# One-hot products that stream four tokens' rows instead of one

## The chip, the cores and the metric

The kernel runs on one core of a Trainium2 chip. A core has TensorE (matrix products, called PE in the profile, with its weight loads counted as PEld), VectorE (DVE), ScalarE (ACT), GpSimd (POOL) and the queue of SyncE (SP), which issues transfers. The metric is the device time of one execution in microseconds; of several runs the median is given.

## The reference

A layer-normalised input `xn` of 2048 tokens by 512 features goes through two branches, whose results are added to the input:

```
xn = layernorm(x)
out = x + attention(xn, wq, wk, wv, wo) + experts(xn, w_q, k1, k2, u, v)
```

The attention has 32 query heads of 16 features and a single key and value head. The expert branch has 32 heads too. For each token and head it scores two sets of 64 keys, takes the two best of each, combines them to four candidates, and keeps the two best of these, so a token picks 64 of 4096 experts with gates `g`:

```
s1 = q1 @ k1.T ; s2 = q2 @ k2.T
top_e, top_s = best 2 of (t1[i] + t2[j]) at expert i1[i] * 64 + i2[j]
g   = softmax(top_s)
act = gelu(xn @ u[top_e])
out = sum over picks of g * act * v[top_e]
```

## The kernel before

The 2048 tokens are four groups of 512. Attention runs through the whole kernel after a start of about 160 us. Its loop (`att_steps`, line 1138) has 280 iterations. Each one issues on TensorE four score products (line 327, tile `sc`), sixteen products with the values (line 341, tile `pv`), four more score products, and then `fill`, which takes work of the expert branch from a generator until a budget per iteration is spent. ScalarE takes an exponential of each pair of score products (line 330, tile `pt`), which the value products of the next iteration need.

The expert branch has two forms. For token groups 0 and 1, the picked rows of `u` and `v` are gathered by GpSimd (line 976), and VectorE takes the dot products (line 988) and adds the weighted rows (line 1023); this runs beside everything else, a fixed few of them in each iteration. For token groups 2 and 3 (`dense`, line 656) there is no gather: the gates of a token are spread out to a dense table over all 4096 experts, and all experts are multiplied by TensorE (lines 733 and 861).

That spreading is where the change lies. An expert's number is split into 128 rows (`oa`) and 32 blocks (`ob`). For each group `q` of `TB = 16` tokens, VectorE makes in `onehot(q)` a table `oa` of shape 128 x 128 x 16 in f16 (line 783), in which one element of each pick and token is 1, and a table `ob` of shape 128 x 32 x 16 in f16 (line 785), which line 786 multiplies by the gates. The partition axis of both holds the picks of a token, 128 of them since each gate is carried in a high and a low part. TensorE then makes for each token one product over the picks: `oa[:, :, i]` is loaded as weights, `ob[:, :, i]` is streamed, 32 rows, and the result is the token's 128 x 32 table of gates in 32 columns of the PSUM tile `p` (tile `pg`, line 815). The innermost axis of both tables is the token, so neighbouring elements of one token lie 16 elements apart. When the 16 tokens of a group are done, ScalarE copies `p` out in two halves (line 820), and transfers take them to DRAM.

The tables are made two groups ahead (`onehot(q + 2)` stands ahead of the products of `q`); `ob` has three buffers, and `oa` shares the eight buffers of the tag `wk`. The PSUM tiles of tag `x` have three buffers. A group of 16 tokens is put down with a cost of 2.0, and an iteration takes up to 4.0 (`MOST`), so most iterations hold two groups. There are 32 groups in each of the two dense token groups, thus 64 in all, and 1024 products on line 815. The order of every engine's instructions is written out by hand (`manual_schedule`), and each engine runs its own in that order.

The results of line 815 are written with `start=True, stop=True`: each product overwrites its output columns and adds to nothing.

## Time and profile before

| | us |
|---|---|
| median of three runs | 1927.19 |
| lowest and highest run | 1919.88, 1936.14 |
| the profiled execution | 1931.19 |
| its span, first to last instruction | 1929.5 |

The profiled execution's mean granted TensorE clock is 0.980. Durations in what follows are from that one execution, whose time is 1.7 us above its span and 4.0 us above the median.

In the lines of the profile an engine's busy time is the union of its instructions' times; since matmuls are pipelined, TensorE counts as busy while a product drains, even if the array does little. PEclk and the column behind the engines in the answers by windows are the granted clock: 1.00 is full speed. The chain of waits follows the work that ended last back in time; its rows are start, length, engine, tile, line and number of instructions. In the rows by line, the first figure behind the bar is busy time in us, the second the mean duration of one instruction in ns, then the idle time just before them.

### The profile page before, as it was taken

What the parts mean: (1) busy time and instruction counts of PE and PEld (TensorE: products, weight loads), DVE (VectorE), ACT (ScalarE), POOL (GpSimd) and SP (SyncE); (2) the same over time, 40 slices, a digit from 0 to 9 for tenths busy, and PEclk for the clock granted to TensorE, in tenths of its full rate; (3) what the DMA queues carried; (4) which work ended last, traced back from release to release, by engine and by line L of the source; (5) the groups of instructions that cost most, each with busy time, mean ns of one, the idle gap of its engine ahead of it and who ended that gap; (6) DMA issues with size and microseconds to landing.
All of it is one profiled execution on the core that took longest, in us unless ns stands there. A gap on an engine that the chain in (4) does not pass through costs nothing.

```text
span 1929.5 us, 35007 instructions
## 1 busy us (share of the span) xinstructions
PE 1865.4 (97%) x10990; PEld 995.2 (52%) x10990; DVE 1633.0 (85%) x6381; ACT 1294.3 (67%) x1803; POOL 693.5 (36%) x920
## 2 busy tenths in 40 slices
PE   6879999999999999999999999999999999999998
PEld 4544444555555544555555454555555555555553
DVE  6626788889998976999999897899988879999994
ACT  3336666655557887877877555555578877888873
POOL 1202334334453213343444354344522124344430
PEclk9989999999999989999999999999999999999999
DMA  7856878887673668799889977877645778899882
GB/s 269 300 202 229 291 263 294 287 294 277 231 268 121 216 213 260 248 283 292 267 288 308 353 278 241 295 243 264 216 138 194 267 222 291 271 284 284 283 274 83
DMA packets 245724, 491.14 MB, mean 255 GB/s; under 512 B 93972, under 2 KB 106260, under 8 KB 245532
## 3 DMA queue, kind: packets, MB, share of 16 engines
q0 software_dynamic: 73728, 268.47, 41.4%
q1 hardware_dynamic: 170568, 219.56, 34.9%
q8 instruction: 88, 1.44, 0.3%
q10 hardware_dynamic: 1236, 0.82, 0.1%
q14 instruction: 104, 0.85, 0.1%
HBM read 427.41 MB, written 56.07 MB: 251 GB/s over the span
## 4 chain that ended last, share of the span: by engine, by line
PE 84%; DVE 3%; ACT 2%; issue 1%; DMA 1%; another core or an unknown queue 0%; SPq 0%; ACTq 0%; DVEq 0%
PE pv L341 23%; PE psc L531 18%; PE sc L327 17%; PE pact L733 10%; PE pout L861 9%; PE pg L815 2%; PE pwo L434 2%; ACT pt L330 2%; PE pw L487 2%; DVE oh L783 1%; DMA wk<-dw 1%; DVE xa L1023 1%; DMA wqt<-in_wqT_dram 0%; PE pwt L494 0%; PE pwl L409 0%
## 5 line engine op out<-in xcount | busy, mean ns | idle before, releaser
L330 ACT ACTIVATE pt<-sc 128x1024 f32<-128x1024 f32 x1024 | 994.4, 1026 | 459.2 <-PE sc L327 405.9
L976 POOL DMA_INDIRECT g<-in_uv_dram,idx x512 | 555.0, 1084 | 1009.5 <-DVE xa L1023 531.9
L341 PE MATMUL pv<-pt,vaug 128*32 128x512 f32 x4096 | 508.9, 615 | 0.0
L531 PE MATMUL psc<-wk,xt 128*128 128x512 f32 x1536 | 390.9, 402 | 6.6 <-DVE wk L497 3.5
L327 PE MATMUL sc<-qa,kaug 64*128 64x512 f32 x2048 | 387.0, 453 | 7.7 <-ACT pt L330 6.9
L1023 DVE SCALAR_TENSOR_TENSOR xa<-g,w,xa 128x512 f32<-128x512 f32 x512 | 371.5, 744 | 0.1
L988 DVE CUSTOM_DVE_ANT_0 g<-g,xa 128x512 f32<-128x512 f32 x512 | 335.2, 680 | 6.6 <-DMA g<-in_uv_dram,idx 6.6
L531 PEld LDWEIGHTS psc<-wk,xt 128*128 128x128 f32 x1536 | 279.4, 189 | 110.5 <-issue 40.3
L327 PEld LDWEIGHTS sc<-qa,kaug 64*128 64x128 f32 x2048 | 157.1, 187 | 326.1 <-ACT pt L330 194.3
L341 PEld LDWEIGHTS pv<-pt,vaug 128*32 128x32 f32 x4096 | 108.8, 111 | 255.7 <-issue 254.1
L546 DVE FIND_INDEX8 i<-m,psc 128x8 uint32<-128x64 f32 x1024 | 206.2, 220 | 0.0
L733 PE MATMUL pact<-xt,wk 128*128 128x512 f32 x768 | 196.0, 400 | 0.0
L861 PE MATMUL pout<-wk,wd 128*128 128x512 f32 x768 | 194.9, 402 | 0.2 <-DVE wd L919 0.2
L544 DVE MAX8 m<-psc 128x8 f32<-128x64 f32 x1024 | 146.1, 213 | 41.2 <-PE psc L531 40.0
L861 PEld LDWEIGHTS pout<-wk,wd 128*128 128x128 f32 x768 | 140.8, 188 | 47.4 <-issue 5.5
L733 PEld LDWEIGHTS pact<-xt,wk 128*128 128x128 f32 x768 | 139.4, 188 | 48.6 <-issue 17.9
L864 DVE TENSOR_TENSOR da<-da,pout 128x512 f32<-128x512 f32 x128 | 82.7, 678 | 10.1 <-PE pout L861 8.6
L698 DVE TENSOR_TENSOR wk<-rw,wk 128x512 fp32r<-128x512 f32 x128 | 84.7, 682 | 7.1 <-ACT wk L697 7.1
L783 DVE TENSOR_TENSOR oh<-oh 128x2048 f16<-128x2048 f16 x64 | 78.0, 1219 | 2.3 <-PE pg L815 1.7
L815 PEld LDWEIGHTS <-oh 128*128 128x128 f16 x1024 | 68.4, 163 | 13.6 <-issue 4.8
L815 PE MATMUL pg<-oh 128*128 128x32 f16 x1024 | 73.7, 246 | 0.8 <-DVE oh L786 0.7
L697 ACT CAST wk<-rw 128x512 fp32r<-128x512 f32 x128 | 74.0, 632 | 0.0
(159 smaller groups left out, 1356.4 us busy)
## 6 DMA issues: line engine op xcount, KB each, us to landing
wk<-dw SPq DMA_DIRECT2D x96, 512.0 KB
wqt<-in_wqT_dram SPq DMA_DIRECT2D x32, 512.0 KB
dw<-wk SPq DMA_DIRECT2D x32, 512.0 KB
rw<-in_ub_dram SPq DMA_DIRECT2D x64, 256.0 KB
rw<-in_vb_dram SPq DMA_DIRECT2D x64, 256.0 KB
gy<-dg SPq DMA_DIRECT2D x64, 256.0 KB
qa<-dqh SPq DMA_DIRECT2D x128, 64.0 KB
g<-in_uv_dram,idx POOLq DMA_INDIRECT x512
```

The costliest lines, as they stand in the source:

```text
L327: nc.tensor.matmul(p[:, b, :], kaug[o:o + 64, kc * P:(kc + 1) * P], QA[u][o:o + 64, i, :], start=True, stop=True)
L330: nc.scalar.activation(pt, p, AF.Exp, scale=SCALE)
L341: nc.tensor.matmul(PV[u][32 * j:32 * j + 32, :], vaug[:, kc, :], pt[:, b, :], start=kc == 0, stop=kc == 15)
L531: nc.tensor.matmul(p, XT[k][:, a, j * P:(j + 1) * P], WC[n_][k][:, bb, :], start=n == 0, stop=n == 11)
L544: nc.vector.max(m8[:, jb, s, :], p[:, s * E:(s + 1) * E])
L546: nc.vector.max_index(i8[:, jb, s, :], m8[:, jb, s, :], p[:, s * E:(s + 1) * E])
L733: nc.tensor.matmul(p, us[:, a, k * P:(k + 1) * P], XT[k][:, c, :], start=n == 0, stop=n == 11)
L815: nc.tensor.matmul(p[:, i * NB:(i + 1) * NB], oa[:, :, i], ob[:, :, i], start=True, stop=True)
L861: nc.tensor.matmul(p, wd[0][:, a, j * P:(j + 1) * P], vs[:, c, :], start=n == 0, stop=n == 5)
L976: nc.gpsimd.indirect_dma_start(out=gt, out_offset=None, in_=uv, in_offset=bass.IndirectOffsetOnAxis(ap=IDX[ph, c, ti][:, s:s + 1], axis=0))
L988: nc.vector.tensor_tensor_reduce(u, u, XN[TPH * ph + ti], scale=1.0, scalar=0.0, op0=OP.mult, op1=OP.add, accum_out=a[:, i:i + 1])
L1023: nc.vector.scalar_tensor_tensor(acc, v, w[:, i:i + 1], acc, op0=OP.mult, op1=OP.add)
```

## The change

Each product of line 815 streams, instead of the 32 rows of its own token, those of its token and of the next three of the group, as far as the group reaches: 128 rows for the first thirteen tokens, then 96, 64 and 32. It writes as many columns of `p`. The columns of the later tokens then hold a product of their `ob` with the wrong `oa`, until the later token's own product, which comes behind on the same engine, overwrites them. After the sixteenth product every token's columns hold its own result, as before.

```diff
+WIDE = 4
...
             p = xtile("pg")
             for i in range(TB):
-                nc.tensor.matmul(p[:, i * NB:(i + 1) * NB], oa[:, :, i], ob[:, :, i], start=True, stop=True)
+                n = min(WIDE, TB - i)
+                nc.tensor.matmul(p[:, i * NB:(i + n) * NB], oa[:, :, i],
+                                 ob[:, :, i:i + n].rearrange("p b t -> p t b"), start=True, stop=True)
             pv_ = p.rearrange("p (t b) -> p b t", b=NB)
```

The order of instructions on every engine is the same in both programs; only the sizes of the products of line 815 differ.

## The prediction

> **What bounds the kernel now.** I read the page first, then the busy time and clock by windows, then the chain of waits through the two stretches in which the changed line runs.

> ```profile
> span 1929.5 us, 35007 instructions
> PE 1865.4 (97%) x10990; PEld 995.2 (52%) x10990; DVE 1633.0 (85%) x6381; ACT 1294.3 (67%) x1803; POOL 693.5 (36%) x920
> PEclk9989999999999989999999999999999999999999
> PE 84%; DVE 3%; ACT 2%; issue 1%; DMA 1%; another core or an unknown queue 0%; SPq 0%; ACTq 0%; DVEq 0%
> L783 DVE TENSOR_TENSOR oh<-oh 128x2048 f16<-128x2048 f16 x64 | 78.0, 1219 | 2.3 <-PE pg L815 1.7
> L815 PEld LDWEIGHTS <-oh 128*128 128x128 f16 x1024 | 68.4, 163 | 13.6 <-issue 4.8
> L815 PE MATMUL pg<-oh 128*128 128x32 f16 x1024 | 73.7, 246 | 0.8 <-DVE oh L786 0.7
> ```

> TensorE carries the kernel (84% of the chain), so a microsecond of its time is nearly a microsecond of the result. The changed line 815 is 1024 pairs of one weight load (128 columns) and one product that streams 32 rows. Tenths of the clock are too coarse, so I asked for windows: columns are length, busy time of PE, PEld, DVE, ACT and POOL, then the granted clock.

> ```profile
> 613.05:715.40 102.35, 100.98 (x923) 53.39 (x922) 93.70 (x194) 87.08 (x146) 21.48 (x18) 0.90 0.63 203
> 1425.40:1532.40 107.00, 102.94 (x940) 54.42 (x939) 96.54 (x198) 90.98 (x152) 24.14 (x20) 0.90 0.63 207
> 740.00:1087.00 347.00, 343.72 (x1933) 186.13 (x1925) 315.80 (x740) 268.07 (x377) 139.81 (x125) 1.00 0.89 284
> ```

> The first two are the stretches from the first to the last one-hot product (the second with the few us behind it); the third is ordinary work. Only there is the clock cut, though the page calls PE busy throughout. A tenth of 102.35 and of 107.00 us is 10.2 and 10.7 us of lost TensorE time, some 20 us in all. Windows of line 815 alone (PE, PEld, clock) show what comes ahead of a cut:

> ```profile
> 633.70:637.10 3.40, 2.42 (x32) 2.19 (x32) 1.00 0.72 220
> 637.10:640.50 3.40, 0.00 (x0) 0.00 (x0) 0.55 0.94 253
> 651.00:654.50 3.50, 2.23 (x32) 2.09 (x32) 1.00 0.97 353
> 654.50:657.90 3.40, 0.00 (x0) 0.00 (x0) 0.50 0.92 362
> ```

> A stretch of 3.4 us that holds 32 of these pairs is followed by one at half the clock. I read it so: whatever grants the clock does not see this work as the page does, because 32 rows per pair leave the array idle for most of a pair.

> Now the chain of waits, one undisturbed iteration and then what a cut does to it, and the ends of both stages:

> ```profile
> 618.46 2.17 PE pg L815 x32
> 620.63 0.67 PE sc L327 x4
> 621.29 1.85 PE pv L341 x16
> 623.14 0.66 PE sc L327 x4
> ...
> 637.77 3.38 PE pv L341 x16
> ...
> 714.25 1.14 PE pg L815 x16
> ```
> ```profile
> 1526.74 0.44 DVE oh L786
> 1527.17 0.04 issue
> 1527.21 1.18 PE pg L815 x16
> 1528.40 1.15 PE sc L327 x3
> 1529.55 2.93 PE pv L341 x16
> ```

> An iteration is 2.17 + 0.67 + 1.85 + 0.66 = 5.35 us of PE. The cut does not fall on the one-hot products but on what comes behind: pv takes 3.38 instead of 1.85 us. Each stage holds 32 groups of 16 pairs. Stage one lasts from 613.05 to 714.25 + 1.14 = 715.39, that is 102.3 us, of which 10 are the clock: PE's own floor is 92 us. Stage two ends differently: its last products begin 0.03 us after the VectorE table that they wait for (line 786).

> So VectorE, which builds the tables, is the second bound. In windows (third figure DVE):

> ```profile
> 613.05:690.00 76.95, 76.18 (x708) 40.72 (x707) 75.32 (x155) 65.77 (x109) 16.99 (x14) 0.91 0.63 200
> 690.00:707.30 17.30, 17.30 (x154) 8.88 (x156) 13.89 (x27) 13.21 (x24) 3.34 (x3) 0.80 0.51 170
> 1428.00:1527.20 99.20, 95.16 (x880) 50.70 (x873) 91.62 (x187) 84.35 (x141) 22.99 (x19) 0.91 0.63 207
> 1528.20:1532.40 4.20, 4.20 (x24) 1.13 (x21) 2.40 (x10) 3.73 (x10) 1.04 (x1) 0.59 0.55 170
> ```

> In stage one VectorE is 98% busy until 690 and its last table is done at 707.3: 94.25 us with 89.2 busy, 5.0 idle. In stage two it is idle 99.20 - 91.62 = 7.6 us. A full clock can take out only such idle time before VectorE sets the pace.

> **The change, part by part.** No instruction is added, removed or moved on any engine, and no wait: a group still has 16 loads and 16 products, the further rows lie in a table that the group waits for already, and the copy behind it still waits for its last product. What changes is that a group streams 13 x 128 + 96 + 64 + 32 = 1856 rows instead of 16 x 32 = 512.

> *The price of the rows.* A pair now takes 2.17 us / 32 = 68 ns. No row of before shows a product of 128 f16 rows, so I bound it:

> ```profile
> L494 PE MATMUL pwt<-ident,wt 128*128 128x128 f32 x128 | 20.0, 285 | 2.3 <-DVE i L546 2.3
> 176.46 0.60 PE L494 MATMUL pwt<-ident,wt 128*128 128x128 f32 x4
> 1102.62 3.70 PE L531 MATMUL psc<-wk,xt 128*128 128x512 f32 x15
> 721.60 3.43 PE pwo L434 x8
> ```

> Line 494 (timeline) streams 128 f32 rows per load: four in 0.60 us, one alone 0.285, so (0.60 - 0.285) / 3 = 105 ns a pair. Line 434 streams 512 f32 rows in 3.43 / 8 = 429 ns, 107 for 128: nearly the same per row, so the load of 128 columns hides under the streaming of the product before. Line 531 streams 512 rows in the reduced type F32R in about 3.70 / 15 = 247 ns, little over half of line 434's: 62 for 128. Below nothing the cost can't be, since loads and products stay the same in number. The bounds are thus 68 ns (the load sets the pace, the rows are free) and 105 ns (each row takes two beats, as f32). The f16 operand, the narrower type, is nearest to line 531, 62 ns, which is just under the 68 that the load takes now; two streams of nearly equal length hardly interlock without loss, so I take 75 ns. Then a group costs 13 x 7 = 91 ns more and the 96-row product a few: 0.1 us, 3 us a stage.

> [...]

> *What the clock returns.* By line 531's rate the array streams 62 of 75 ns of a pair instead of 15 of 68, so a 3.4 us stretch full of pairs should look nearly as busy as one full of pv, which the 347 us window shows at 1.00. I expect all or nearly all cuts in the two stages to go. The cover is lost where VectorE comes next:

> - Stage one: 10 us of PE time come back, 3 are paid: PE would end 7 us earlier, at about 708. VectorE's last table could be done at 707.3 - 5.0 = 702.3, so it does not stop that. Gain 7.
> - Stage two: VectorE's idle time is the limit, 7.6 us, and behind its last table the 4.2 us at a clock of 0.59 lose 1.7. Of the 7.6 the two long waits are surely owed to the late PE: VectorE waits for a tanh of ScalarE, which stands in its queue behind exponentials that wait for scores.

> ```profile
> 1449.64 0.16 DVE L1011 SCALAR_TENSOR_TENSOR w<-gth,ga 128x4 f32<-128x4 f32 x1 [3.03 <-ACT gth L1004]
> 1480.94 0.16 DVE L1011 SCALAR_TENSOR_TENSOR w<-gth,ga 128x4 f32<-128x4 f32 x1 [2.24 <-ACT gth L1004]
> ```

> 3.03 + 2.24 + 1.7 = 7.0; from that I take off 1 for the dearer pairs ahead of those waits. Gain 6.

> Sum: 13 us off the profiled execution, 1931.19 to 1918; that execution lies 4.0 us above the median of the runs (1927.19), so the forecast for the median is 1914. What is won stays won: behind both stages the chain is PE again. If pairs stay at 68 ns, the gain is 10 and up to 7.6 + 1.7 = 9.3, together 19: 1908. [...]

> **The rivals.**

> *Rows read slowly (slower than before).* The rows of the moving table lie 16 f16 apart, 32 bytes, while lines 494, 434 and 531 stream rows that lie side by side. If each row then takes two beats, a pair takes 105 ns: 13 x 37 + 11 = 0.49 us a group, 16 us a stage. Stage one: 16 - 10 = +6; stage two: a PE floor of 92 + 16 = 108 against 102.8 + 1.7 now: +3.5. Together +9.5, 1937. At three beats (158 ns, 13 x 90 + 61 = 1.23 us a group, 39 a stage) +29 and 131 - 104.5 = +27: 1983. It decides from where the extra PE time of a stage passes the 10 us that the clock returns: about 23 ns a product, a pair of 91 ns. Against it: the weights are read at that same step of 32 bytes, 128 of them in at most the 68 ns of a pair. For it: no row shows the moving side at this step with more than 32 rows. [...] Chance 0.12 for two beats, 0.08 for three or more.

> *The clock stays as it is.* If what grants the clock weighs something else than streamed rows (the values, most of them zero, or pauses between instructions), the cuts remain and 0 to 6 us of dearer pairs are partly hidden under VectorE: 1927 to 1931. For it: 613 to 634 holds iterations full of pairs with no cut, so the threshold is near and its measure not known. Chance 0.15.

> *All of it comes back* at 68 ns a pair, 1908 or a little lower: part of the forecast's own range.

> **How the numbers follow.** Forecast (clock restored, pairs below 85 ns) 0.65, its own range 1907 to 1920; clock stays 0.15; slow rows 0.20. The runs of before spread over 1919.88 to 1936.14, so 1% (19 us) is about what can be told from no change. Faster by over 1% is below 1907.9: only the forecast's best end and the spread of runs, 0.14. Slower by over 1% is above 1946.5: three beats, and the upper part of the two-beat case, 0.13. The rest, 0.73, is within 1%. The range 1906 to 1942 leaves out the three-beat case, the upper end of two beats and a little below: under 0.2.

> **What would show it.** Right: windows over the two stages show a clock of 0.98 or more; pv in the chain stays at 1.85 us; a group of 32 pairs takes 2.2 to 2.5 us; line 815 waits for VectorE more often, with VectorE 97% busy or more in both stages; stage one ends about 7 us and stage two 13 us earlier against the start of the span. Wrong: 32 pairs in 3.4 us or more (slow rows), or a clock of 0.90 again (something else is weighed); or both as forecast and yet no shorter span, which would mean that VectorE or ScalarE had bound the stages all along.

## The result: a tenth slower

The changed kernel takes 2120.35 us (2119.46 to 2124.21) against 1931.66 in the runs beside it. The two medians are 1.098 to each other; the ratio over all these runs is 1.0993, interval 1.0962 to 1.1025. The profiled execution took 2119.46 us, its span is 2117.7. The page of the changed kernel, where the one-hot product stands on line 817 (815 before) and other lines are one to three higher:

```profile
span 2117.7 us, 35007 instructions
PE 2060.2 (97%) x10990; PEld 1081.4 (51%) x10990; DVE 1635.5 (77%) x6381; ACT 1298.8 (61%) x1803; POOL 694.5 (33%) x920
PEclk9989999999987769999999999999967689999999
PE 88%; DMA 2%; ACT 1%; DVE 1%; issue 1%; SPq 0%; ACTq 0%; DVEq 0%
L817 PE MATMUL pg<-oh 128*128 128x128 f16 (+3 forms) x1024 | 230.2, 400 | 0.1
L817 PEld LDWEIGHTS <-oh 128*128 128x128 f16 x1024 | 145.7, 149 | 91.7 <-issue 10.5
```

Nothing but line 817 is dearer as work: DVE, ACT and POOL are busy for as long as before, to within 5 us. The clock is worse, not better, in two places. Windows from the first to the last one-hot product of each stage (length, then PE, PEld, DVE, ACT, POOL, then clock), first before, then after:

```profile
613.05:715.30 102.25, 100.88 (x923) 53.29 (x922) 93.60 (x194) 86.98 (x145) 21.48 (x18) 0.90 0.63 203
1425.40:1528.30 102.90, 98.84 (x920) 53.33 (x919) 94.24 (x189) 87.35 (x144) 23.20 (x20) 0.92 0.63 208
```
```profile
612.50:810.20 197.70, 197.70 (x923) 96.67 (x921) 96.76 (x199) 90.73 (x147) 21.24 (x18) 0.72 0.34 105
1518.40:1716.40 198.00, 198.00 (x920) 96.78 (x919) 97.46 (x196) 89.78 (x145) 24.24 (x20) 0.72 0.34 112
```

The stages grew from 205.2 to 395.7 us, by 190.5; the span grew by 188.2. So the whole loss lies there, in the 1024 products and what runs among them, and VectorE, busy for 92% of each stage before, has half of it free. One iteration in the chain of waits of the changed kernel, and who waited for line 817 (us, times; line 786 is 785 before, the blocks' table):

```profile
612.55 7.09 PE pg L817 x32
619.64 1.15 PE sc L328 x4
620.79 3.50 PE pv L342 x16
624.29 0.66 PE sc L328 x4
```
```profile
  DVE oh L786: 72.4, 17
  ACT gst L823: 50.6, 29
```

Thirty-two pairs take 7.09 us instead of 2.17. With 16 such in a stage that is 16 x 4.92 = 79 us of the 95.5 that a stage grew by. The rest is the clock, which stands at 0.72 over the stage. The pairs take no longer for it, as the next table shows; what is behind them pays, pv with 3.50 us for 1.85 and the scores with 1.15 for 0.66. Over the first stage pv was busy for 53.2 us instead of 41.5, and the scores for 34.3 instead of 27.3. VectorE now waits for TensorE to free its tables.

The time of one product, from the end of one to the end of the next, by the records of the trace (median over the 64 groups, in ns):

```
rows of the product    128   96   64   32
changed kernel         240  183  123   60
kernel before            -    -    -   65
```

That is nearly a straight line through nothing: 1.87 to 1.92 ns a row. The granted clock made no difference to it: products of 128 rows took 240 ns at full clock and 239 at half.

### The profile page after: what moved, and what is told of

It is laid out like the page before. It is cut to its first block, busy times and chain, and to the rows that moved or that the text cites. A ratio compares the mean times of both kernels' runs of the same rounds, so it can differ in the third digit from the quotient of the medians.

```text
span 2117.7 us, 35007 instructions
## 1 busy us (share of the span) xinstructions
PE 2060.2 (97%) x10990; PEld 1081.4 (51%) x10990; DVE 1635.5 (77%) x6381; ACT 1298.8 (61%) x1803; POOL 694.5 (33%) x920
## 4 chain that ended last, share of the span: by engine, by line
PE 88%; DMA 2%; ACT 1%; DVE 1%; issue 1%; SPq 0%; ACTq 0%; DVEq 0%
PE pv L342 24%; PE psc L532 17%; PE sc L328 16%; PE pg L817 11%; PE pact L734 8%; PE pout L864 8%; PE pwo L435 2%; PE pw L488 1%; ACT pt L331 1%; DMA wqt<-in_wqT_dram 1%; DMA wk<-dw 1%; DMA gy<-dg 0%; PE pwt L495 0%; PE pwl L410 0%; PE pwl L418 0%
## 5 line engine op out<-in xcount | busy, mean ns | idle before, releaser
L331 ACT ACTIVATE pt<-sc 128x1024 f32<-128x1024 f32 x1024 | 993.8, 1024 | 584.9 <-PE sc L328 531.1
L342 PE MATMUL pv<-pt,vaug 128*32 128x512 f32 x4096 | 535.8, 643 | 0.0
L328 PE MATMUL sc<-qa,kaug 64*128 64x512 f32 x2048 | 397.9, 467 | 3.5 <-ACT pt L331 2.8
L328 PEld LDWEIGHTS sc<-qa,kaug 64*128 64x128 f32 x2048 | 162.9, 195 | 328.4 <-ACT pt L331 173.3
L817 PE MATMUL pg<-oh 128*128 128x128 f16 (+3 forms) x1024 | 230.2, 400 | 0.1
L817 PEld LDWEIGHTS <-oh 128*128 128x128 f16 x1024 | 145.7, 149 | 91.7 <-issue 10.5
L1014 DVE SCALAR_TENSOR_TENSOR w<-gth,ga 128x4 f32<-128x4 f32 x128 | 20.6, 161 | 126.9 <-ACT gth L1007 126.8
L784 DVE TENSOR_TENSOR oh<-oh 128x2048 f16<-128x2048 f16 x64 | 78.1, 1220 | 42.1 <-PE pg L817 41.5
L699 DVE TENSOR_TENSOR wk<-rw,wk 128x512 fp32r<-128x512 f32 x128 | 85.0, 684 | 18.2 <-ACT wk L698 13.5
```

The lines of the kernel that those rows point to most:

```text
L328: nc.tensor.matmul(p[:, b, :], kaug[o:o + 64, kc * P:(kc + 1) * P], QA[u][o:o + 64, i, :], start=True, stop=True)
L331: nc.scalar.activation(pt, p, AF.Exp, scale=SCALE)
L342: nc.tensor.matmul(PV[u][32 * j:32 * j + 32, :], vaug[:, kc, :], pt[:, b, :], start=kc == 0, stop=kc == 15)
L817: nc.tensor.matmul(p[:, i * NB:(i + n) * NB], oa[:, :, i], ob[:, :, i:i + n].rearrange("p b t -> p t b"), start=True, stop=True)
```

## The experiments

The theory from these figures was that the price belongs to the step of 32 bytes between streamed rows. Its rivals were that 128 rows of f16 behind a load, or columns written twice, cost that much however they lie (R1), or that the load at a step does it (R2).

**Neighbouring rows, up to 128 of them.**

```diff
-ob[:, :, i:i + n].rearrange("p b t -> p t b")
+ob.rearrange("p b t -> p (b t)")[:, i * NB:(i + n) * NB]
```

> As the changed kernel (up to 128 rows a product), but the streamed rows are 128 neighbouring elements of the same table ob instead of elements 32 bytes apart; the products are thus formed with other gates than the reference's. Theory S (each streamed row that lies 32 bytes from the one before costs about 240/128 = 1.87 ns, whatever the clock): a pair falls from 240 to 60 to 80 ns, 32 pairs from 7.1 us to 2.0 to 2.6, the clock in both stages is restored to 0.97 or more, and the time is 1905 to 1932, at or under that of before. Rival R1 (128 rows of f16 behind a load, or columns that are written again by the next product, are slow as such): 32 pairs stay at about 7.1 us and the time at 2120. Rival R2 (the weights' own step of 32 bytes makes the pair slow): as R1, since the weights are unchanged.

1913.8 us against 1923.22 for the kernel before in the runs beside it, 0.9947 (0.9928 to 0.9967). Its two stages by windows, and one run of 32 pairs in its timeline (start, length):

```profile
611.80:706.50 94.70, 90.00 (x922) 52.33 (x921) 93.19 (x194) 86.85 (x146) 21.43 (x18) 1.00 0.63 210
1415.20:1511.50 96.30, 90.01 (x920) 52.22 (x919) 93.92 (x189) 87.46 (x145) 23.39 (x20) 1.00 0.68 221
```
```profile
643.76 2.19 PE L817 MATMUL pg<-oh 128*128 128x128 f16 x32
```

The same rows in number, the same weights, the same overwritten columns, and a pair takes 62 to 65 ns (48 to 50 for the last three of a group, which stream fewer rows). The clock is 1.00 in both stages. R1 and R2 fall. VectorE is busy for 98% of both stages, so it is what now sets their length.

**The kernel's own elements, token innermost.** The four tokens of a row block are read side by side, and the PSUM tile is laid out likewise.

```diff
-nc.tensor.matmul(p[:, i * NB:(i + n) * NB], oa[:, :, i],
-                 ob[:, :, i:i + n].rearrange("p b t -> p t b"), start=True, stop=True)
-pv_ = p.rearrange("p (t b) -> p b t", b=NB)
+nc.tensor.matmul(p.rearrange("p (b t) -> p b t", t=TB)[:, :, i:i + n], oa[:, :, i],
+                 ob[:, :, i:i + n], start=True, stop=True)
+pv_ = p.rearrange("p (b t) -> p b t", t=TB)
```

> As the changed kernel, with the same elements streamed in another order: token innermost, so four rows lie side by side in 8 bytes and the next four 32 bytes further; the PSUM tile holds the token innermost too, so a product writes four neighbouring columns and then steps 64 bytes. Theory S with a price per 32-byte step and not per row: 32 steps a product, as before the change, so a pair of 60 to 75 ns, a clock of 0.97 or more in both stages, 1905 to 1932. If each row costs 1.87 ns as soon as the operand isn't one run: a pair of 240, 2120. Rival R1: 240 and 2120. If the stepped writes into PSUM cost something: a pair between 80 and 240.

1918.09 us, 0.9963 (0.9939 to 0.9986): a little faster than before, with the clock at 1.00 in the stages. But 32 pairs take 2.68 us in the chain (2.75 in the timeline) and not 2.2.

```profile
606.87 2.68 PE pg L817 x32
610.22 1.85 PE pv L342 x16
```

The mean hides a pattern. By the place of the token in its group, the products take (median, ns; tokens 1 to 15):

```
token           1   2   3   4   5   6   7   8   9  10  11  12  13  14  15
token inner    86  60  82  61 123 119 124  67  83  58  83  61  66  64  62
```

Tokens 5, 6 and 7 are those whose four elements, 8 bytes, cross a border of 16 bytes. This gave theory L: the price is 1.87 ns for each 16-byte line touched, not for each row.

**Thirty-two neighbouring rows.** The kernel before with the operand of the first experiment (`WIDE = 1`).

> As the kernel before (32 rows a product), but the 32 rows are neighbouring elements of ob; the products are formed with other gates than the reference's. Theory S: in the kernel before, too, the rows set the pair (32 x 1.87 = 60 ns of 65), so it falls to what the load takes, 40 to 62 ns; fewer rows' time in a window, so the clock in the stages stays at 0.88 to 0.93; VectorE binds, so the time is 1915 to 1932. Rival (the load of 128 columns sets the pair of before): 65 ns, no change at all.

1911.75 us, 0.9940 (0.9922 to 0.9958). All its 15 products of a group take 61 to 62 ns, so that is what a pair with a load of 128 columns, 32 bytes apart, takes when the rows cost little; I put it down to the load, which is an estimate, since no run has cheap rows behind any other load. The clock stays cut:

```profile
605.50:701.40 95.90, 94.01 (x923) 51.61 (x921) 93.14 (x194) 86.67 (x145) 21.44 (x18) 0.95 0.65 211
1410.90:1509.70 98.80, 95.34 (x922) 51.75 (x921) 94.15 (x189) 87.15 (x144) 23.43 (x20) 0.93 0.67 216
```

The pair was as expected. The clock of the first stage, 0.95, lies above the range given, 0.88 to 0.93, and the time 3 us under its own. Beside the first experiment this is about what the rest of the clock is worth: 194.7 us for the two stages against 191.0, since VectorE needs 187 in both. The timed runs don't show this difference: 0.9940 here and 0.9947 there, with intervals that overlap.

**Neighbouring weights, 32 rows at the step.**

```diff
-oa[:, :, i]
+oa.rearrange("p a t -> p (a t)")[:, i * P:(i + 1) * P]
```

> As the kernel before, but the weights of a product are 128 neighbouring elements of oa instead of elements 32 bytes apart; the products are formed with other one-hot rows than the reference's. Theory S: the rows set the pair, so it stays at 60 to 65 ns and the time at 1920 to 1937. Rival R2 (the load at a step sets the pair): it falls to 55 ns or less.

1915.37 us in one run, 5 us under the range given. Every product takes 60 ns, 32 x 1.87: that is the price of the rows at a step, and the load can take no longer than that here. R2, which has 55 ns or less, falls for the kernel before too.

```profile
640.50 2.08 PE L817 MATMUL pg<-oh 128*128 128x32 f16 x32
```

In the kernel before, rows (60 ns) and load (62 ns by that estimate) were thus nearly equal, and a pair of 65 took 3 to 5 ns more than either.

**Token innermost, no line crossed.** As the second, with `n = min(WIDE, 8 - i % 8)`.

> As the kernel with the token innermost, but no product reaches past the eighth or sixteenth token of its group, so the four neighbouring elements (8 bytes) of a step never cross a 16-byte border; a product streams 128, 96, 64 or 32 rows. Theory L (the price is 1.87 ns for each 16-byte line that a product touches, whatever the number of rows in it): the products of tokens 5, 6 and 7, at 120 ns there with 64 lines, fall to 60 to 67, 32 pairs from 2.68 us to about 2.2, the clock stays at 0.98 or more in both stages, and the time is 1908 to 1918, 0.3 to 0.8% under that of before. Rival (the 120 ns have another cause, such as the PSUM columns that they write): they stay, 2.6 us, 1915 to 1920.

1914.1 us against 1921.73, 0.9956 (0.9936 to 0.9976). That this is faster than the second experiment, at 0.9963, is not shown: the intervals overlap.

```profile
610.00:705.00 95.00, 93.24 (x923) 54.35 (x921) 93.32 (x194) 87.34 (x146) 21.46 (x18) 1.00 0.65 210
1417.30:1514.00 96.70, 93.02 (x920) 54.45 (x919) 94.07 (x189) 87.65 (x145) 23.45 (x20) 1.00 0.68 222
```
```profile
642.57 2.40 PE L817 MATMUL pg<-oh 128*128 128x128 f16 x32
```

Tokens 5, 6 and 7 fell to 62 to 65 ns, as theory L has it. Thirty-two pairs take 2.4 to 2.5 us and not 2.2, because tokens 1, 3, 9 and 11 stay at 83 to 86. It costs nothing: VectorE is busy for 98 and 97% of the stages.

**Read as there, written side by side.** The second experiment's operand with the changed kernel's output `p[:, i * NB:(i + n) * NB]`.

> The rows are read as in the kernel with the token innermost, but written to neighbouring columns of PSUM; the columns stand in an order that the copy behind does not expect, so the gates reach other experts than in the reference. Theory L: tokens 5, 6 and 7 stay at 120 ns. The 83 ns of tokens 1, 3, 9 and 11: if they come from writing pairs of columns that start at an odd one, they fall to 60 to 65; if from reading at an odd element, they stay.

```
token           1   2   3   4   5   6   7   8   9  10  11  12  13  14  15
written aside  67  67  64  67 124 121 122  68  64  69  65  68  70  66  61
```

The time was 1917.54 us in one run. The border of the read keeps its price (tokens 5 to 7), and the odd tokens fall from 83 to 86 to 64 to 67 ns. So that part came from writing: four f32 columns that start at an odd one, 64 bytes apart. From an even one the same step cost nothing (58 to 62 ns for tokens 2, 4, 10 and 12). An odd start thus cost some 20 ns for 128 columns; why it does, no run shows.

**Rows 8 bytes apart, and 16.** From the start of `ob`, with a step of 4 elements (up to 128 rows) and of 8 (64 rows, `WIDE = 2`).

```diff
-ob[:, :, i:i + n].rearrange("p b t -> p t b")
+ob.rearrange("p b t -> p (b t)")[:, 0:n * NB * 4:4]
```

> As the changed kernel, but a product streams 128, 96, 64 or 32 rows that lie 4 elements (8 bytes) apart, from the start of ob; the gates are thus not those of the reference. 128 rows touch 64 lines of 16 bytes. Theory L: 120 ns for 128 rows, 90 for 96, then 60 to 62 (the load); 32 pairs in 3.6 us, some 1940 to 1965. Rival (two rows in a line are enough for full speed): 55 to 67 ns, 1908 to 1925. Rival (each row at a step costs 1.87 ns): 240, 2120.

> A product streams 64 rows (the last one 32) that lie 8 elements (16 bytes) apart, from the start of ob; the gates are not those of the reference. 64 rows touch 64 lines. Theory L: 120 ns a pair, as 64 rows 32 bytes apart (123); 32 pairs in 3.8 us, some 1945 to 1975. Rival (the price belongs to the step of 32 bytes and grows with it): half of that, 60 to 65 ns, 1908 to 1925.

1950.06 and 1992.4 us, one run each. Their products by rows (median, ns), with the changed kernel's again:

```
bytes between rows   128 rows   96   64   32
 8                        120   96   61   33
16                          -    -  122   60
32                        240  183  123   60
```

Two rows in a 16-byte line cost half as much a row, and one row in a line costs the same at 16 bytes as at 32. In lines, 64 take 120 to 123 ns, 48 take 96, 32 take 60 to 61 and 16 take 33: 1.87 ns a line for the longer products, up to 2.1 for the shortest. The expected 90 ns for 96 rows was 6 short, and the load did not hold the last product at 60. The time of the second, 1992, lies above the range given (1945 to 1975), and the reason is in its clock, by windows over the stages; first the step of 16 bytes, then that of 8:

```profile
610.60:744.10 133.50, 133.50 (x923) 80.98 (x921) 94.66 (x195) 88.93 (x147) 21.45 (x18) 0.85 0.49 156
1454.80:1590.40 135.60, 135.12 (x920) 81.60 (x919) 96.95 (x196) 89.45 (x145) 24.12 (x20) 0.84 0.50 163
```
```profile
611.40:724.70 113.30, 113.30 (x923) 75.36 (x922) 94.30 (x195) 88.84 (x147) 21.45 (x18) 1.00 0.56 183
1433.50:1547.80 114.30, 113.69 (x920) 75.33 (x919) 96.30 (x196) 89.26 (x145) 24.12 (x20) 1.00 0.59 192
```

At the step of 8 bytes the clock is whole, at 16 it is cut by 15%; the last section comes back to it.

## Why the prediction was wrong

The step that failed is one term of the sum, the price of the rows. The prediction said: "The f16 operand, the narrower type, is nearest to line 531, 62 ns, which is just under the 68 that the load takes now; ... so I take 75 ns", between bounds of 68 and 105. A product of 128 rows took 240. That f32 takes two beats a row was my reading of 105 ns, and the loss of two streams that interlock was an estimate too: no row of before showed either, and of a loss the experiments show only the 3 to 5 ns in a pair of 65. All three rows that I bounded it with stream operands whose elements lie side by side, so none of them was near, and 105 was no upper bound. The nearest row was line 815 itself. I took its 68 ns for the load's price and its 32 rows for free; the experiments show that the rows needed 60 of them. Read so, four times the rows gives four times 60 ns, which is what was measured. Nothing in the trace of before separated the two, and where a time has two claimants, four times the work of one of them has to be bounded by four times the whole: 4 x 68 = 272 ns a pair, or 13 x 204 + 136 + 68 ns = 2.86 us a group, 91 us a stage. That bound belonged in the range.

The rival of rows read slowly named the right cause, and its turning point (a pair of 91 ns) was passed at once. Its sign, 32 pairs in 3.4 us or more, appeared with 7.09. But it was stopped at 105 and 158 ns a pair, and given little chance on this ground: "the weights are read at that same step of 32 bytes, 128 of them in at most the 68 ns of a pair." The weights are read so (a pair of 62 ns with cheap rows), and it says nothing of the rows: a line costs the load at most 62 / 128 = 0.48 ns there, and the moving operand 1.87. With a line for each row 128 rows took 240 ns, with two rows in a line still 120, and with eight no more than the 62 to 65 of a pair.

*The clock.* "I expect all or nearly all cuts in the two stages to go" failed with the first step and not by itself. Where the wide products were fast, in the first, second and fifth experiments, the clock was 1.00 in both stages. In the changed kernel the rows come hardly denser in time than before: 3712 rows for 32 pairs in 7.16 us are 0.52 a ns, against 1024 in 2.23 us, 0.46. And runs of pairs three times as long fill more stretches of 3.4 us: 31 to nine tenths or more, and none before. The rival that the clock stays as it is, with something other than streamed rows being weighed, is not borne out.

*VectorE as the second bound, and the gain of 13 us.* Both came out where the pairs cost what the prediction had put them at. With the clock restored and a pair of 63 to 75 ns the two stages took 191.0 us (neighbouring rows) and 191.7 (no line crossed), 14.2 and 13.5 less than 205.2, with VectorE at 97 to 98%. In the latter the pairs are dearer than before (2.40 us for 32 against 2.23), so the gain is the clock's. Its timed comparison shows less, 0.9956, about 8 us: the execution that was profiled before the change, 1931.19 us, lay high among its runs. That the 13 us were met this closely is thus in part luck. Nor is a whole clock the only way there: with 32 neighbouring rows the stages took 194.7 us at 0.95 and 0.93, and the timed runs gained as much.

*No instruction moved and no wait added* was right as well, and the new waits (VectorE, 72.4 us for free tables) come from durations alone.

## What to carry to other kernels

Before streaming more of an operand through TensorE, count the 16-byte lines that its rows touch, and let the innermost axis of the stream run along memory: the same elements in another order, with no line crossed, took 60 to 86 ns instead of 240. Where two costs overlap in the one duration that the trace has, bound a change of either by the whole. A stretch of small products that is followed by a cut clock can be filled with rows that are overwritten later, and that is worth only what the next engine leaves: here 0.4% of the time. Rows that lie side by side from the start gained 0.6% here with nothing to fill; a kernel that builds its table so, and computes the reference, was not run.

## What the runs showed of the hardware

```
kernel                       us    rows   rows/ns   clock
before                      2.23   1024    0.46     0.90 0.92
32 neighbouring rows        2.15   1024    0.48     0.95 0.93
neighbouring weights        2.08   1024    0.49     0.93 0.93
64 rows, 16 bytes apart     3.97   1984    0.50     0.85 0.84
changed                     7.16   3712    0.52     0.72 0.72
128 rows, 8 bytes apart     3.74   3712    0.99     1.00 1.00
token innermost             2.75   3712    1.35     1.00 1.00
no line crossed             2.40   3328    1.39     1.00 1.00
written side by side        2.66   3712    1.40     1.00 1.00
neighbouring rows           2.19   3712    1.69     1.00 1.00
```

At 0.46 to 0.52 rows a ns the clock was cut in every stage, and most where the runs of pairs were longest; from 0.99 on it never was. The two steps of 8 and 16 bytes show it best, with runs of nearly equal length. Where between 0.52 and 0.99 it turns wasn't tried. By what the clock is granted, no run shows. In the traces of the kernel before and of the changed one, the cuts in the stages, each to 0.5, last 3413 ns or two or three times that. In the changed kernel 31 stretches of that length were filled to nine tenths or more with one-hot pairs, and each was followed by a cut; at the step of 8 bytes there were 14, and none was. Pairs that follow without a gap can thus be followed by half the clock when their rows come slowly, here 0.52 a ns.
- A product that wrote four neighbouring PSUM columns every 64 bytes took some 20 ns more when it began at an odd column (83 to 86 ns, against 64 to 67 for the same rows written side by side), and nothing more when it began at an even one (58 to 62).
